# A fused local attention and MLP kernel: value tiles padded to 128 rows, one DMA for regrouped probabilities, and another order of work

## The chip, the cores and the metric

The kernel runs on one core of a Trainium2 chip. A core has five engines with instruction queues of their own: PE (TensorE, matrix products; its weight loads are listed apart as PEld), DVE (VectorE), ACT (ScalarE), POOL (GpSimd) and SP (SyncE, which here issues nearly all DMAs). Each engine works its queue in order; semaphores tie the queues together. The metric is the time of one execution on the device in microseconds (us); lower is better. Tiles in SBUF have up to 128 rows ("partitions"); PSUM holds what PE produces.

## The reference

Inputs are q, k and v (4 batches, 8 heads, 768 positions, 64 features) and two weight matrices. Attention sees a band of 31 positions around each query and, beside it, 24 block summaries (the maximum of each 32 keys, the mean of each 32 values). The result goes through an MLP with a gate of its own; all arithmetic is to float32 accuracy.

```python
k_sum = k.reshape(B, H, nb, block, D).max(axis=3)        # block = 32, nb = 24
v_sum = v.reshape(B, H, nb, block, D).mean(axis=3)
scores_l = scale * np.matmul(q, k.transpose(0, 1, 3, 2)) # kept where |i - j| < 16
scores_s = scale * np.einsum('bhsd,bhnd->bhsn', q, k_sum) + np.log(block)
a = softmax(concatenate([scores_l, scores_s]))           # with 1e-9 in the divisor
attn_out = np.matmul(a, concatenate([v, v_sum], axis=2))
x = attn_out.transpose(0, 2, 1, 3).reshape(B * S, H * D) # 3072 x 512
h = x @ w_in                                             # 512 x 2048
out = (h * erf(softplus(h))) @ w_out                     # 2048 x 512
```

## The kernel before, in words

**Tiling.** The 3072 tokens go in 6 chunks of 512. The unit of attention is a *quad*: one chunk and one pair of heads, so 24 quads, numbered `qd`. A quad has 8 groups of 64 queries; each group sees a window of 96 positions (`LW`) and 24 block sums (`NS`), 120 columns (`NK`) in all. For each quad: `scores` (PE), `softmax` (DVE: maxima and normalization; ACT: exponentials), `transp` (the probabilities are turned so that keys lie on the rows), `av` (PE: the product with the value tile `vw`), and a split of the result x into a high and a low half (`xsplit`, tiles `xh` and `xl`), since PE multiplies float32 as three products of such halves.

**Value tiles.** `vw` has 120 rows: 96 of the window, loaded from `v_win`, and 24 with the block sums (`vsum`), copied in on the chip. Quads 0 to 3 have tiles of their own (`vwf`): `load_vw_first` loads them, and the block sums come in by a copy on ACT (quad 0), by a DMA (quad 1), and by two copies on ACT that ride behind the first weight cast (`spread`, quads 2 and 3). Later quads share one tile `vw`: `load_quad_v` issues the load and, behind it on SP, one or two DMAs with the sums.

**Turning the probabilities.** Quads 0 to 7 are turned by PE and copied by ACT (`ptr`). From quad 8 on, DVE transposes blocks of 32 x 32 (`blocks`, L666), a DMA writes the result to DRAM (`out_`, L670), and four DMAs, each for 32 (the last for 24) rows, read it back regrouped (`back`, L676, tile `ptd`).

**MLP.** 24 periods (`k`), four for each chunk: `mm1` (first layer; from period 8 on replaced by `products`, which needs seven products in place of eight), softplus and erf on ACT, the gate and its split on DVE (`gsplit`), `mm2` (second layer). Weights come packed as 64-bit words and are converted at the start by three DVE operations a unit (`convert`: `a`, `b`, `c`), a cast on ACT and a subtraction on DVE (`split`: high and low half of `w`). Later, halves are kept in DRAM and read again (`w<-dr`, `ws<-ds`).

**What sets the order.** Nothing is issued as it is written. Every piece of work is entered into a plan (`P.add`) with the engines that may do it, its assumed length, and what it reads and writes. `Plan.order` then goes through time by these assumptions: on the engine that is free first it takes, of the ready pieces, the one with the smallest key, which is its due time plus a number from the table `TUNE`; a third entry picks a table set of ACT, a fourth ties a piece to one engine. DMAs are pieces of SP. The resulting sequence is issued engine by engine; waits on semaphores come from what each piece reads and writes. Before the weights are there, `busy` fills PE with matmuls on zeros (tile `idle`), at the places of the table `FILL`, after seven at the start.

**The order at the start.** PE's queue has a score piece for each of the first four quads, the block sums of V (`vs`), turns and products of the four quads, and 48 matmuls of `mm1` of period 0, 12 for each quad, which need that quad's `xh` and `xl`. DVE has the block maxima of the keys (`ksum`), the row maxima of the scores (L615) and their product with -0.125 (L631), which the exponentials (L621) need.

## Time and profile before

| what | value |
|---|---|
| time, 3 runs | 607.96, 608.32, 609.86 us; median 608.32 us |
| the profiled execution | 608.67 us, its span 606.9 us |
| PE, PEld busy | 599.3 us (99%), 498.8 us (82%) |
| DVE, ACT busy | 445.9 us (73%), 410.8 us (68%) |
| granted PE clock, mean | 0.997 |
| DMA | 166.29 MB, mean 274 GB/s |

The span runs from the first to the last instruction of one profiled execution; the time beside it also has what lies around the span. A group row has busy time, mean ns of one instruction and, behind the second bar, the idle time of the engine just before and what ended it. Busy PE time counts matmuls from issue to modelled end, so it overlaps and says little on how well PE is used. A chain row is a step on the way back from the last instruction. Line numbers are those of the kernel before; in the changed kernel the same code stands up to ten lines earlier or two later.

### The profile page before, as it was taken

The page shows a single profiled execution, that of the slowest core. Times are in us where ns is not written, and L with a number is a line of the kernel's source. Part 1 is how long each engine was busy: PE and PEld are TensorE (multiplying, and loading weights), DVE is VectorE, ACT ScalarE, POOL GpSimd, SP SyncE. Part 2 cuts the span into 40 slices and gives each one's busy share as a digit, 9 for nine tenths or more (in the row PEclk, how much of TensorE's full clock was granted, in tenths as well). Part 3 has the DMA queues.
Part 4 walks back from the last instruction along what each step waited for, and adds up shares of the span by engine and source line. Part 5 has one row for each costly group of instructions (what it writes and reads, how often), then busy time and mean ns, then how long its engine had stood idle before and what let it go on. Part 6 is the DMA issues. An engine that isn't in the chain of part 4 may idle for free.

```text
span 606.9 us, 12143 instructions
## 1 busy us (share of the span) xinstructions
PE 599.3 (99%) x4722; PEld 498.8 (82%) x4722; DVE 445.9 (73%) x910; ACT 410.8 (68%) x819; POOL 3.9 (1%) x28
## 2 busy tenths in 40 slices
PE   9899999999999999999999999999999999999997
PEld 5576566778888889889799899899898899899886
DVE  4999999977998897765979758659558547544442
ACT  5978889899968885873766964656854433542670
POOL 2000000000000000000000000000000000000000
PEclk9899999999999999999999999999999999999999
DMA  8999768759798999998989999999987773675512
GB/s 324 276 362 312 286 215 289 282 180 316 256 297 309 322 313 329 301 320 302 312 310 277 385 315 294 310 312 308 319 302 230 278 237 140 245 245 193 218 70 69
DMA packets 47380, 166.29 MB, mean 274 GB/s; under 512 B 5148, under 2 KB 17884, under 8 KB 34780
## 3 DMA queue, kind: packets, MB, share of 16 engines
q1 hardware_dynamic: 46748, 165.01, 80.3%
q8 instruction: 37, 0.61, 0.4%
q10 hardware_dynamic: 576, 0.52, 0.3%
q14 instruction: 19, 0.16, 0.1%
HBM read 131.99 MB, written 31.46 MB: 269 GB/s over the span
## 4 chain that ended last, share of the span: by engine, by line
PE 93%; DMA 6%; SPq 0%; issue 0%; DVE 0%; ACT 0%; DVEq 0%
PE ops L962 39%; PE h L807 15%; PE hb L848 15%; PE ha L848 11%; PE ops L958 5%; PE px L704 3%; PE pA L581 3%; DMA vwf<-v_win 2%; DMA dt<-ot 2%; PE px L701 2%; DMA kf<-k_nat 1%; PE pA L653 1%; DMA ptd<-dt 1%; PE idle L999 0%; PE vt L464 0%
## 5 line engine op out<-in xcount | busy, mean ns | idle before, releaser
L962 PE MATMUL ops<-w,gh 128*128 128x512 f32 x704 | 227.8, 393 | 0.0
L962 PEld LDWEIGHTS ops<-w,gh 128*128 128x128 f32 x704 | 132.5, 188 | 28.4 <-issue 1.0
L962 PE MATMUL ops<-w,gl 128*128 128x512 f32 x352 | 137.5, 391 | 0.0
L1212 ACT ACT_TABLE_LOAD x91 | 116.8, 1283 | 1.6
L938 DVE TENSOR_TENSOR hc<-wt,hc 128x1024 f32<-128x1024 f32 x44 | 52.9, 1222 | 64.9 <-ACT wt L926 64.8
L807 PE MATMUL h<-xh,w 128*128 128x512 f32 x256 | 88.6, 408 | 0.0
L279 ACT COPY hc<-hb 128x256 f32<-128x256 f32 x57 | 21.1, 371 | 97.8 <-PE hb L848 41.7
L962 PEld LDWEIGHTS ops<-w,gl 128*128 128x128 f32 x352 | 66.2, 188 | 12.4
L621 ACT ACTIVATE prx<-prx,stats 128x120 f32<-128x120 f32 x160 | 61.0, 382 | 4.1 <-DVE stats L609 3.8
L807 PEld LDWEIGHTS h<-xh,w 128*128 128x128 f32 x256 | 48.1, 188 | 12.6 <-issue 1.6
L848 PE MATMUL hb<-w,ws 128*128 128x256 f32 x384 | 56.5, 283 | 0.0
L945 DVE TENSOR_TENSOR gl<-hc,gh 128x1024 fp32r<-128x1024 f32 x44 | 53.7, 1220 | 0.7
L848 PEld LDWEIGHTS hb<-w,ws 128*128 128x128 f32 x384 | 50.8, 192 | 0.2
L807 PE MATMUL h<-xl,w 128*128 128x512 f32 x128 | 50.1, 391 | 0.0
L926 ACT ACTIVATE wt<-wt 128x1024 f32<-128x1024 f32 x48 | 49.7, 1057 | 0.4
L914 ACT ACTIVATE wt<-hc 128x1024 f32<-128x1024 f32 x32 | 32.8, 1054 | 5.6 <-DVE hc L279 5.3
L279 DVE CAST gh<-hc 128x1024 fp32r<-128x1024 f32 x38 | 26.2, 691 | 11.0 <-PE ops L962 10.5
L621 ACT ACTIVATION_READ_ACCUMULATOR prx<-prx,stats 128x1 f32 x160 | 29.9, 187 | 0.0
L958 PE MATMUL ops<-a32s,gw 128*128 128x512 f32 x64 | 29.6, 597 | 0.0
L807 PEld LDWEIGHTS h<-xl,w 128*128 128x128 f32 x128 | 24.1, 188 | 6.2 <-issue 1.4
L848 PE MATMUL ha<-w,ws 128*128 128x256 f32 x192 | 28.3, 283 | 0.0
L848 PE MATMUL ha<-xh,ws 128*128 128x256 f32 x128 | 28.2, 283 | 0.0
(167 smaller groups left out, 995.9 us busy)
## 6 DMA issues: line engine op xcount, KB each, us to landing
w<-dr SPq DMA_DIRECT2D x36, 1024.0 KB
ws<-ds SPq DMA_DIRECT2D x30, 1024.0 KB
kw<-k_win SPq DMA_DIRECT2D x20, 480.0 KB
rw<-w_in SPq DMA_DIRECT2D x8, 1024.0 KB
rw<-w_out SPq DMA_DIRECT2D x8, 1024.0 KB
dr<-w SPq DMA_DIRECT2D x8, 1024.0 KB
dt<-ot SPq DMA_DIRECT2D x16, 512.0 KB
ds<-ws SPq DMA_DIRECT2D x8, 1024.0 KB
```

The source lines that it names most:

```text
L279: e.copy(o, i) if e is nc.scalar else e.tensor_copy(o, i)
L581: nc.tensor.matmul(s["sc"][a][o, n:n + rhs.shape[-1]], lhsT=s["qb"][r, 64 * j:64 * j + 64], rhs=rhs, start=qd >= MQ, stop=True, skip_group ...
L621: nc.scalar.activation(s["pr"][:, j], s["pr"][:, j] if qd >= MQ else s["sc"][j // NI][:, i * NK:(i + 1) * NK], AF.Exp, scale=-1.0 if qd >= ...
L807: nc.tensor.matmul(hs[k, f][:, 0:T], lhsT=w[m], rhs=xt[ch, cc][x], start=(cc == 0 and n == 0), stop=(cc == 3 and n == 2))
L848: nc.tensor.matmul(shape, lhsT=w[m], rhs=y[l], start=first and c == 0 and i == 0, stop=c == 1 and i == 2, skip_group_check=True)
L914: nc.scalar.activation(wt[k, n], hc[k, n], AF.Softplus)
L926: act(0.96, lambda n=n: nc.scalar.activation(wt[k, n], wt[k, n], AF.Erf, scale=-1.0 if k < SOFT else 1.0), [s], [s], table=("sig",), after ...
L938: e.tensor_tensor(hc[k, n], wt.pop((k, n)), hc[k, n], op=ALU.mult)
L945: e.tensor_tensor(gs[k, n][1], hc.pop((k, n)), f32(gs[k, n][0]), op=ALU.subtract)
L958: nc.tensor.matmul(os_[ch, t], lhsT=x[0][:, i % 2, t * 128:(t + 1) * 128], rhs=w32["o", g, i // 2][:, i % 2], start=first, stop=last)
L962: nc.tensor.matmul(os_[ch, t], lhsT=x[y][:, i % 2, t * 128:(t + 1) * 128], rhs=w[m], start=first and n == 0, stop=last and n == 2)
L1212: nc.scalar.preload_act_table_set(sets[o["load"]])
```

## The change

1. **Value tiles of 128 rows.** `v_win` is padded with zeros on the host to 128 rows; `vwf` and `vw` have 128 rows and are loaded by DMAs over all of them. `av` reads the first 120. Since the load now writes the rows of the block sums too, what copies the sums in waits for the load. For quads 0 to 3 that is a copy on ACT (or DVE, for quad 0), or an SP DMA if the plan finds it earlier; `spread` is gone.
2. **One DMA back.** `blocks` reads the probabilities with a step of four columns, so that the four blocks interleave, and the tile comes back from DRAM by one DMA over 128 rows in place of four.
3. **Pieces joined.** The row maxima and their product with -0.125 are one piece of the plan; so are the addition of 1e-9 and the reciprocal.
4. **The plan.** The first loads get assumed times of their own (`first_dma`); the assumed landing time (`land`) counts for SP's pieces; the table `TUNE` is another one (it shows as one line below). `FILL` is gone: the fillers follow from the gaps that the plan assumes.

```diff
-TUNE = {0: (-9699.962, 1.5, 0, None), 1: (-9787.921, 1.5, 0, None), 2: (-9784.159, 1.5, 0, None),
...
-FILL = {30: 3, 48: 2, 79: 1, 81: 6, 93: 5, 91: 1, 111: 1}
+TUNE = {1: (0.9682263, 1.5, 0, None), 6: (-6.605486, 1.5, 0, None), 7: (0.7812648, 1.5, 0, None),
...
-            if e == "ACT":
+            if e == "SP":
                 end += o["land"]
...
+    def first_dma(us, fn, r=(), w=(), **kw):
+        return P.add({"SP": us}, lambda e: fn(), r, w, hold=2.0, land=-1.0, **kw)
...
-        dma(1112, go, w=[f"w{n}"])
+        if u in units[:4]:
+            first_dma(2.6, go, w=[f"w{n}"])
+        else:
+            dma(1112, go, w=[f"w{n}"])
...
-            if u == units[0]:
-                spread(2)
-                spread(3)
...
-    vws = [slot(n, [NK, 2, NB, 128], F32, "vwf") for n in W_SLOTS]
+    vws = [slot(n, [128, 2, NB, 128], F32, "vwf") for n in W_SLOTS]
...
-        dma(585, lambda: nc.sync.dma_start(out=st[p]["vw"][0:LW], in_=v_win[0, p]), w=[f"vwf{p}"])
+        first_dma(1.3, lambda: nc.sync.dma_start(out=st[p]["vw"], in_=v_win[0, p]), w=[f"vwf{p}"])
...
+        def rows_(e, p):
+            o, i = st[p]["vw"][LW:NK], vsum[LW:NK, p:p + 1, :].to_broadcast([NS, NB, 128])
+            e.dma_start(out=o, in_=i) if e is nc.sync else copy(e, o, i)
         for p in range(NP):
-            if p == 0:
-                on({"DVE": 1.13, "ACT": 0.95}, lambda e: copy(e, st[0]["vw"][LW:NK], vsum[LW:NK, 0:1, :].to_broadcast([NS, NB, 128])), ["vsum00"], ["vwg0"])
-            else:
-
-                dma(100, lambda p=p: p == 1 and nc.sync.dma_start(out=st[p]["vw"][LW:NK], in_=vsum[LW:NK, p:p + 1, :].to_broadcast([NS, NB, 128])), [f"vsum0{p}"], [f"vwg{p}"])
+            on({"ACT": 0.95, "SP": 0.45} if p else {"DVE": 1.13, "ACT": 0.95}, lambda e, p=p: rows_(e, p), [f"vsum0{p}", f"vwf{p}"], [f"vwg{p}"])
...
-            s["vw"] = sb([NK, NB, 128], F32, "vw")
-            nc.sync.dma_start(out=s["vw"][0:LW], in_=v_win[ch, p])
+            s["vw"] = sb([128, NB, 128], F32, "vw")
+            nc.sync.dma_start(out=s["vw"], in_=v_win[ch, p])
...
+            e.tensor_scalar(s["mx"], s["mx"], -0.125, None, op0=ALU.mult)
...
+            e.reciprocal(s["rs"], s["rs"])
...
-            on({"DVE": 1.14}, red, banks, [f"mx{par}"])
-            on({"DVE": 0.07}, lambda e: e.tensor_scalar(s["mx"], s["mx"], -0.125, None, op0=ALU.mult), [f"mx{par}"], [f"mx{par}"])
+            on({"DVE": 1.3}, red, banks, [f"mx{par}"])
...
-            e.transpose(out=s["ot"].rearrange("p k j q -> p j k q"), in_=prx.rearrange("p j (k q) -> p j k q", k=4))
+            e.transpose(out=s["ot"].rearrange("p k j q -> p j k q"), in_=prx.rearrange("p j (q k) -> p j k q", k=4))
...
-            for k in range(4):
-                n = min(32, NK - 32 * k)
-                e.dma_start(out=s["pt"][32 * k:32 * k + n].rearrange("p a j q -> p a (j q)"), in_=s["dt"][:, 0:n, k].rearrange("a p f -> p a f"))
+            e.dma_start(out=s["pt"].rearrange("p a j q -> p a (j q)"), in_=s["dt"].rearrange("a p k f -> (p k) a f"))
...
-                        nc.tensor.matmul(xo[r, o], lhsT=s["vw"][:, j, r], rhs=s["pt"][:, j % 2, b:b + 64], start=True, stop=True)
+                        nc.tensor.matmul(xo[r, o], lhsT=s["vw"][0:NK, j, r], rhs=s["pt"][0:NK, j % 2, b:b + 64], start=True, stop=True)
...
-                busy(FILL.get(o["n"], 0))
+                busy(int(max(0.0, o["start"] - last) / 0.31))
...
-    v_win = np.ascontiguousarray(windows(v).transpose(0, 2, 4, 1, 3, 5)).reshape(NCH, NP, LW, NB, 128)
+    v_win = np.zeros((NCH, NP, 128, NB, 128), dtype=f)
+    v_win[:, :, :LW] = windows(v).transpose(0, 2, 4, 1, 3, 5).reshape(NCH, NP, LW, NB, 128)
```

How the order moves, at the places that matter at the start. **SP, the first loads**, before (`kf`, `qf`: keys and queries of a quad; `vt`: V by tokens, for its block sums; `rw`: a packed unit of weights):

```order
L495 DMA vt<-v_tok 128x3x512
L490 DMA kf<-k_nat 128x768
L491 DMA qf<-q_t 128x512
L315 DMA rw<-w_in 128x2048
L498 DMA vwf<-v_win 96x1024
L315 DMA rw<-w_in 128x2048
L498 DMA vwf<-v_win 96x1024
L519 DMA vwf<-vsum 24x8x128
L315 DMA rw<-w_in 128x2048
L498 DMA vwf<-v_win 96x1024
```

Ahead of these rows stand, in this order, `qf`, `kf`, `qf`, `kf`, `vt`, `kf`, `qf`. With the change:

```order
L491 DMA kf<-k_nat 128x768 x2
L492 DMA qf<-q_t 128x512
L496 DMA vt<-v_tok 128x3x512 x2
L317 DMA rw<-w_in 128x2048
L499 DMA vwf<-v_win 128x1024
L492 DMA qf<-q_t 128x512
L499 DMA vwf<-v_win 128x1024
L317 DMA rw<-w_in 128x2048
L499 DMA vwf<-v_win 128x1024
L317 DMA rw<-w_in 128x2048 x2
L499 DMA vwf<-v_win 128x1024
```

Ahead of these rows stand `kf`, `qf`, `kf`, `qf`. A key load is first now, the third transfer is the second key load (the fourth before), the last query load stands behind the first `vwf`, the second `vwf` ahead of the second `rw`, and no copy of block sums stands in between.

**ACT, from the third quad's exponentials on**, before (`vwf<-vsum`: block sums into a value tile; `ptr`: turned probabilities; `w<-a`: weight cast; `xh`: high half of x):

```order
L511 COPY vsum<-vs 24x512
L279 COPY vwf<-vsum 24x1024
L658 COPY ptr<-pA 120x512
L658 COPY ptr<-pB 120x512
L621 ACTIVATE prf,stats<-h_302,stats 128x120 x4
L621 ACTIVATE prf,stats<-h_303,stats 128x120 x4
```

And with the change:

```order
L512 COPY vsum<-vs 24x512
L281 COPY vwf<-vsum 24x1024
L651 COPY ptr<-pA 120x512
L651 COPY ptr<-pB 120x512
L281 CAST w<-a_320 128x1024
L281 COPY vwf<-vsum 24x1024
L281 CAST xh<-px 128x512
L615 ACTIVATE prf,stats<-h_322,stats 128x120 x4
```

The first weight cast, the second value tile's sums and quad 0's high half now stand ahead of quad 3's exponentials.

**DVE, the first rows**, before and with the change (`ksum`: block maxima of the keys; `stats<-h`, `stats<-pA`: row maxima of the scores; the TENSOR_SCALAR: the product with -0.125):

```order
L501 TENSOR_REDUCE ksum<-kf 128x24 x2
L615 TENSOR_REDUCE stats<-h_140 128x4
L615 TENSOR_REDUCE stats<-h_141 128x4
L615 TENSOR_REDUCE stats<-pA 128x4
L615 TENSOR_REDUCE stats<-pB 128x4
L631 TENSOR_SCALAR stats<-stats 128x8 x2
```

```order
L502 TENSOR_REDUCE ksum<-kf 128x24 x2
L608 TENSOR_REDUCE stats<-pA 128x4
L608 TENSOR_REDUCE stats<-pB 128x4
L609 TENSOR_SCALAR stats<-stats 128x8
L502 TENSOR_REDUCE ksum<-kf 128x24
```

The product of the first quad stood behind the maxima of two quads; now it follows its own.

More of the change, by code (lines that the diff above doesn't have):

```diff
@@ L489, in load_qk_first @@
         st[p] = dict(qb=qfs[:, p], vw=vws[p // 2][:, p % 2])
-        dma(480, lambda: nc.sync.dma_start(out=kfirst[p], in_=k_nat[0, p]), w=[f"kf{p}"])
-        dma(330, lambda: nc.sync.dma_start(out=qfs[:, p], in_=q_t[0, p]), w=[f"qf{p}"])
+        first_dma(0.97, lambda: nc.sync.dma_start(out=kfirst[p], in_=k_nat[0, p]), w=[f"kf{p}"])
+        first_dma(0.66, lambda: nc.sync.dma_start(out=qfs[:, p], in_=q_t[0, p]), w=[f"qf{p}"])
     def load_v_first():
         for n in range(2):
-            dma(786, lambda n=n: nc.sync.dma_start(out=vts[n], in_=v_tok[3 * n:3 * n + 3].rearrange("t s c -> s t c")), w=[f"vt{n}"])
+            first_dma(2.0, lambda n=n: nc.sync.dma_start(out=vts[n], in_=v_tok[3 * n:3 * n + 3].rearrange("t s c -> s t c")), w=[f"vt{n}"])
     def load_vw_first(p):
-        dma(585, lambda: nc.sync.dma_start(out=st[p]["vw"][0:LW], in_=v_win[0, p]), w=[f"vwf{p}"])
+        first_dma(1.3, lambda: nc.sync.dma_start(out=st[p]["vw"], in_=v_win[0, p]), w=[f"vwf{p}"])
     def ksum_first(p):
@@ L629, in softmax @@
         else:
-            on({"DVE": 1.14}, red, banks, [f"mx{par}"])
-            on({"DVE": 0.07}, lambda e: e.tensor_scalar(s["mx"], s["mx"], -0.125, None, op0=ALU.mult), [f"mx{par}"], [f"mx{par}"])
+            on({"DVE": 1.3}, red, banks, [f"mx{par}"])
         s["exps"] = act(3.02 if qd >= MQ else 2.7, exps, [f"mx{par}"] + ([pr] if qd >= MQ else list(banks)), [pr, f"sm{par}"], table=("log", "exp"))
-        on({"DVE": 0.07}, plus, [f"sm{par}"], [f"rs{par}"])
-        on({"DVE": 0.11}, lambda e: e.reciprocal(s["rs"], s["rs"]), [f"rs{par}"], [f"rs{par}"])
+        on({"DVE": 0.21}, plus, [f"sm{par}"], [f"rs{par}"])
         def norm(e):
@@ L673, in back @@
             s["pt"] = sb([128, 4, 2 * NI, 32], F32, "ptd", "pt")
-            for k in range(4):
-                n = min(32, NK - 32 * k)
-                e.dma_start(out=s["pt"][32 * k:32 * k + n].rearrange("p a j q -> p a (j q)"), in_=s["dt"][:, 0:n, k].rearrange("a p f -> p a f"))
+            e.dma_start(out=s["pt"].rearrange("p a j q -> p a (j q)"), in_=s["dt"].rearrange("a p k f -> (p k) a f"))
         on({"DVE": 1.14}, blocks, [pr], ["ot"])
-        on({"SP": 1.43}, out_, ["ot"], [f"dt{qd % 2}"], hold=0.3, land=3.6)
-        on({"SP": 3.0}, back, [f"dt{qd % 2}"], ["pt"], hold=0.3, land=3.0)
+        on({"SP": 1.43}, out_, ["ot"], [f"dt{qd % 2}"], hold=0.3, land=0.6)
+        on({"SP": 1.9}, back, [f"dt{qd % 2}"], ["pt"], hold=0.3, land=0.4)
     turned = [0]
@@ L692, in go @@
         def go():
-            assert qd >= NP or qd in filled
             xo = s["xo"] = ps("px", bank)
@@ L700, in go @@
                         b = 64 * (NI * a + j // 2)
-                        nc.tensor.matmul(xo[r, o], lhsT=s["vw"][:, j, r], rhs=s["pt"][:, j % 2, b:b + 64], start=True, stop=True)
+                        nc.tensor.matmul(xo[r, o], lhsT=s["vw"][0:NK, j, r], rhs=s["pt"][0:NK, j % 2, b:b + 64], start=True, stop=True)
                     else:
                         z = 2 * (j % 2)
-                        nc.tensor.matmul(xo[r, o].rearrange("d (a q) -> d a q", a=2), lhsT=s["vw"][:, j, r], rhs=s["pt"][0:NK, z:z + 2, NI * a + j // 2], start=True, stop=True)
+                        nc.tensor.matmul(xo[r, o].rearrange("d (a q) -> d a q", a=2), lhsT=s["vw"][0:NK, j, r], rhs=s["pt"][0:NK, z:z + 2, NI * a + j // 2], start=True, stop=True)
         pe(1.08, go, ["pt", "vw"] if qd >= NP else ["pt", f"vwf{qd}", f"vwg{qd}"], [bank])
@@ L1204, in block_attention_mlp @@
     sets = {"exp": "exp_and_others", "log": "natural_log_exp_and_others", "sig": "sigmoid_and_others", "soft": "softplus"}
-    filling = True
+    filling, last = True, free["PE"]
     for o in plan:
@@ L1209, in block_attention_mlp @@
             if filling:
-                busy(FILL.get(o["n"], 0))
+                busy(int(max(0.0, o["start"] - last) / 0.31))
+            last = o["end"]
         if "load" in o:
```

8 lines of the change are left out of this document (1 added, 7 removed).

## The prediction, made before the result was known

> **What bounds the kernel now.** I read the page first (busy time by engine), then a table of stretches, then the chain of waits, then the instructions of the first 42 us engine by engine. The page, and the stretches (start:end, length, then busy us of PE, PEld, DVE, ACT and POOL with their counts, the granted PE clock, the DMA engines' share, GB/s):
>
> ```profile
> PE 599.3 (99%) x4722; PEld 498.8 (82%) x4722; DVE 445.9 (73%) x910; ACT 410.8 (68%) x819; POOL 3.9 (1%) x28
> ...
> 0.00:16.00 16.00, 14.88 (x242) 8.35 (x243) 7.54 (x18) 8.45 (x35) 3.86 (x28) 1.00 0.90 328
> 16.00:36.00 20.00, 18.35 (x265) 12.67 (x264) 18.93 (x28) 18.44 (x58) 0.00 (x0) 0.91 1.02 273
> 36.00:50.00 14.00, 13.94 (x115) 10.74 (x113) 13.48 (x16) 9.47 (x12) 0.00 (x0) 1.00 1.01 402
> 50.00:120.00 70.00, 70.00 (x471) 45.15 (x462) 69.27 (x140) 61.82 (x125) 0.00 (x0) 1.00 0.79 274
> 120.00:228.00 108.00, 108.00 (x750) 87.53 (x747) 95.00 (x196) 93.03 (x168) 0.00 (x0) 1.00 0.82 282
> 318.00:603.00 285.00, 285.00 (x2140) 255.50 (x2136) 175.26 (x361) 160.40 (x296) 0.00 (x0) 1.00 0.75 251
> ```
>
> Two limits follow each other. From 318 us PE alone is the bound (DVE 175 of 285 us). From 16 to 120 us DVE is busy too: 18.93 of 20, 13.48 of 14, 69.27 of 70 us. In the first 16 us DVE works 7.54 us only. So what the start loses on DVE stays lost: PE cannot make it up later. A busy PE is not a useful PE either; the chain of waits (start, us, what) tells more:
>
> ```profile
> 7.42 14.17 DMA vwf<-v_win
> 22.43 1.12 issue
> 23.55 0.80 PE px L701 x19
> ...
> 29.71 4.10 PE h L807 x18
> ...
> 35.51 2.94 PE h L807 x12
> ...
> 39.67 1.58 PE h L807 x6
> 41.49 7.74 PE h L807 x33
> 50.21 0.91 PE h L807 x3
> ...
> 581.47 21.80 PE ops L962 x96
> ```
>
> The start hangs on the first window load of V. The gap of 1 us at 49.2 is one of several before 228 us. The last row gives PE's true price: 21.80 / 96 = 0.227 us a matmul; the tail behind it (603.27 to 606.9) keeps its form.
>
> **The start, step by step.** DVE and ACT now (start, us, what; in brackets the idle time and what ended it):
>
> ```profile
> 4.51 0.95 DVE L501 TENSOR_REDUCE ksum<-kf 128x24 f32<-128x768 f32 x1 [3.37 <-DMA kf<-k_nat]
> 7.43 0.95 DVE L501 TENSOR_REDUCE ksum<-kf 128x24 f32<-128x768 f32 x1 [1.97 <-DMA kf<-k_nat]
> 8.30 1.21 DVE L615 TENSOR_REDUCE stats<-h 128x4 f32<-128x480 f32 x2
> 10.55 0.29 DVE L631 TENSOR_SCALAR stats<-stats 128x8 f32<-128x8 f32 x2
> 20.12 0.69 DVE L332 TENSOR_SCALAR a<-rw 128x1024 uint32<-128x1024 uint32 x1
> 25.98 0.69 DVE L332 TENSOR_SCALAR a<-rw 128x1024 uint32<-128x1024 uint32 x1 [0.90 <-DMA rw<-w_in]
> 37.41 1.22 DVE L357 TENSOR_TENSOR w<-a,w 128x1024 fp32r<-128x1024 f32 x1
> 38.55 1.22 DVE L335 SCALAR_TENSOR_TENSOR a<-rw,a 128x1024 uint32<-128x1024 uint32 x1
> 39.80 1.23 DVE L338 SCALAR_TENSOR_TENSOR a<-rw,a 128x1024 uint32<-128x1024 uint32 x1
> 40.94 0.68 DVE L720 TENSOR_TENSOR xl<-px,xh 128x512 fp32r<-128x512 f32 x1
> ...
> 10.81 0.36 ACT L621 ACTIVATE prf<-h,stats 128x120 f32<-128x120 f32 x1 [6.36 <-DVE stats L631]
> 19.18 0.58 ACT L511 COPY vsum<-vs 24x512 f32<-24x512 f32 x1
> 19.79 1.04 ACT L279 COPY vwf<-vsum 24x1024 f32<-24x1024 f32 x1
> ```
>
> The first exponentials wait for the multiplication by -0.125 at 10.55, which stands behind both quads' maxima (8.30 to 10.5). Everything after them (24 exponentials up to the copy at 19.18, 2.7 us a quad, then transposes) is late with them, and DVE starts converting weights at 20.12.
>
> **Maxima and key loads.** The multiplication now follows its own quad's maxima, and the key load that holds DVE is the third transfer, not the fourth. Bytes decide when that lands: 1.31 MB stood up to it, now 1.05 MB. At the first row's rate, with nothing in the first 2 us and about 300 GB/s to 6 us, 1.05 MB is moved at 5.2 us; a landing is seen 0.6 to 1.3 us after its bytes (the loads seen at 4.51 and 7.43 had 0.66 and 1.31 MB up to them, moved at 3.9 and 6.1), I take 1.0: 6.2 us. Then a reduction (0.9), two maxima (1.15) and the product (0.15): exponentials from 8.4, 2.4 us earlier. Three quads take them to 16.6, the copy of the V sums to 17.2. The folded pairs of small operations remain the same instructions: nothing.
>
> **The V load.** SP's issues now:
>
> ```profile
> 7.42 0.35 SPq L498 DMA_DIRECT2D vwf<-v_win  x1
> 19.78 0.98 SPq L519 DMA_DIRECT2D vwf<-vsum  x1
> ...
> 14.00:16.00 2.00, 2.00 (x16) 1.02 (x11) 1.84 (x5) 2.00 (x14) 0.00 (x0) 1.00 1.07 422
> 22.00:24.00 2.00, 0.88 (x25) 0.79 (x25) 2.00 (x4) 2.00 (x13) 0.00 (x0) 1.00 1.07 246
> 24.00:26.00 2.00, 2.00 (x31) 1.28 (x26) 1.10 (x3) 1.46 (x8) 0.00 (x0) 0.62 0.99 276
> ```
>
> Up to the first weight unit 5.24 MB are issued, all over 128 partitions, and 328 GB/s x 16 us = 5.25 MB: it has just arrived when the first 96-row V load's turn comes. From there to 36 us the engines are as busy (1.02) but move 273 GB/s, and beyond 36 us, with the V loads through, 402 again. In these 20 us the four V loads (1.57 MB) share 5.46 MB; at 0.41 MB/us these take 13.3, so 6.7 us are lost, 1.7 per V load. I therefore price a 128-row load by its bytes at 0.41 MB/us (0.52 MB, 1.3 us); the other end is 273 GB/s for everything, as now.
>
> Up to the first V load the new order issues 5.51 MB: moved at 16.6, seen at 17.6 instead of 21.6. The second (6.29 MB) is seen at 19.5, the weight units 0 to 3 (4.98, 7.34, 8.91, 9.96 MB) at 16.4, 22.0, 25.7, 28.2. SP no longer waits for the sums (its copy stood at 19.78).
>
> **What the padding costs on ACT.** The load now fills the rows of the sums too, so the four copies of the sums must wait for it, on ACT, in order. Behind the first copy stand the two copies of the transposed probabilities, and PE's first product waits for those. ACT is free at 17.2, waits to 17.6, copies to 18.7 and 19.7. PE has its scores of quad 3 done by 19.5 (the last query load, 5.77 MB, is seen at 18.2), so the product runs 19.8 to 20.9; now it starts behind the load, at 21.6, and ends at 24.4. ACT pays one copy more (1.04 us), inside this sum.
>
> **The sum at 42 us.** DVE can convert from 16.4 (weight unit 0 seen; its two normalizations end at 15.5), not from 20.12. From there to the last low half of x (xl of quad 3) it has, by the pitches of the rows above, four conversions (0.6 + 1.25 + 1.14 each, 12.0 us), three low halves of weights (1.14 each, 3.4), four of x (0.6 each, 2.4), a cast of x (0.6), normalization, maxima and small ones (2.8), and two block sums of the next batch (1.7) that now come later: 22.9 us without a wait, since ACT's inputs come 0.4 to 1.6 us ahead of each use. It ends at 39.3, now at 41.6 (the row at 40.94), and is 1.7 us of other work ahead: DVE leads by 4.0 us. PE's row for the wait behind that half:
>
> ```profile
> 41.68 0.50 PE L807 MATMUL h<-xl,w 128*128 128x512 f32 x1
> ```
>
> All 36 matmuls that need nothing of quad 3 are done before it (the 18, 12 and 6 of the chain). In the new order they are too: the products of quads 0 to 3 end at 20.9, 27.5, 33.0 and 37.3, and the 36 at 39.3 (on ACT the exponentials of quad 3 end at 25.1, the copies for quad 1 at 26.1, a normalization and a weight cast at 29.6, the copies for quads 2 and 3 at 30.6 and 35.3; a product needs 1.1 us behind its copies, that of quad 3 also nine matmuls ahead of it, of which three wait for quad 2's half). So PE is 2.4 us ahead at the same point, DVE 4.0. Until 120 us both are full; there the 1.6 us that DVE is further ahead can close gaps of PE like the one at 49.2, half of it I count: 2.4 + 0.8 = 3.2 us.
>
> **The clock.** 26 filling matmuls become 18. After 20 to 24 us, where PE worked 2.41 of 4 us with no gap over 1.2 us, the clock fell to 0.62. My PE is idle for 1.7 us before the scores of quad 3, and as sparse up to 24. The cost lies between nothing (PE waits for ACT and DVE anyway) and 3 us (PE's 3 us there at half speed, and some 13 matmuls); 0.5 taken, near the lower end, since DVE sets the pace. [...]
>
> **Steady work.** Three edits, each hidden. The rows are a stretch while the regrouped probabilities come back in four partial loads, the issues of these, the only PE wait for them, the transposes, and SP's longest wait:
>
> ```profile
> 328.00:329.00 1.00, 1.00 (x10) 1.00 (x10) 1.00 (x2) 0.54 (x2) 0.00 (x0) 1.00 1.07 148
> 324.63 1.71 SPq L676 DMA_DIRECT2D ptd<-dt  x4
> PE px L704 <- DMA ptd<-dt: 1.1, 1, 1.1
> L666 DVE STREAM_TRANSPOSE ot<-prx x16: 1233/1238/1246, 132.8 to 468.3; 128x1024 f32<-128x1024 f32 x16
> SPq L381 <- PE ops L962: 88.9, 19, 6.5
> ```
>
> One load over all partitions saves SP about 1.3 us a quad and lifts a dip of 148 GB/s; PE waited 1.1 us once, so 0 to -1.1, and 0 taken, as a new order can put such a wait elsewhere. The transposes read with a step of four elements, which no row shows; conversions that read every second word cost 1.2 us like plain ones. The bounds are nothing and a doubling, the distance between the two forms of conversion (0.69 and 1.22 us for the same 1024 elements): up to 16 x 1.24 = 19.8 us, which lies in DVE's idle 13 us (120 to 228) and 110 us (318 to 603); without that cover it would be paid in full. The copies of the sums behind each V load now wait on SP for it (20 times), with weight reloads and query and key loads behind them, which PE waits for. One landing is 1.3 + 1.0 us, on a queue that waits 88.9 us for PE to free weight buffers: 0 on the path, 1 us at most in all. 0.13 MB more per V load (20 times) is 6 us at 0.41 MB/us, in a DMA share of 0.75.
>
> Sum: -3.2 + 0.5 = -2.7 us. The profiled execution took 608.67 us (span 606.9), 0.35 over the median of 608.32; against the median the forecast is 605.6.
>
> **The rivals.** (1) *The padding does not speed the load.* For: the slow stretch also holds a 24-row copy of the sums, which I cannot separate from the loads. Against: the rate returns as the V loads end. At 273 GB/s the weight units 1 to 3 are seen at 24.7, 30.4, 34.3, DVE waits 3 us for them and xl of quad 3 ends at 42.9, 1.3 later than now, with 1.7 of block sums done ahead: at worst 1.3 lost on PE, half of DVE's 0.4 regained, less than 0.3%: 608.8 with nothing else moved, no change. [...]
>
> (2) *ACT is held: slower.* If the slow stretch goes by bytes and a padded load is a third longer there, 5.6 us (16 to 21.6) become 7.5 and the first V load is seen at 23.5. ACT, in order, holds both transposed copies, and everything behind moves by 5.9 us less the 0.4 us spare: 3.2 - 5.5 = 2.3 lost, 610.6. The gain is gone from a landing at 21.2 on. Against: the same as for (1).
>
> (3) *More comes with it.* The gaps before 228 us (like that at 49.2) arise where DVE is full; with 4.0 us of DVE's lead passed on whole, that gap of 1.0 closed and the 1.1 us wait with it, 6.1 us go: 602.2.
>
> **How the numbers follow.** A measurement of this kernel can tell about 0.3% (1.8 us) from no change. The forecast 0.50 (its own range 603.2 to 606.4), (3) 0.16, (1) 0.22, (2) 0.12. Faster is the forecast and (3), 0.66; same is (1), 0.22; slower is (2), 0.12. The range 601 to 609 holds the forecast with the clock's 3 us, (1), and (3) with the clock's half us back and some more; it leaves (2) out.
>
> **What would show it.** Exponentials from about 8.4; first V load seen before 18.5; about 400 GB/s from 16 to 28 us; DVE converting from about 16.5; xl of quad 3 ending near 39.3; a granted clock near 1 there; transposes between 1.24 and 2.5 us; PE from 318 us as before. It is wrong if ACT waits over 4 us for the first V load, if DVE waits for weights, or if a lead of over 2 us at 42 us is there and PE gives it back before 318.

## The result, and the profile after

The changed kernel takes 613.41 us (median of 5 executions, 611.56 to 613.56), the kernel before, beside it on the same chip, 608.32 (607.47 to 610.76): a ratio of 1.0066 worked out from all executions (the medians alone would give 1.0084), 95% interval 1.0038 to 1.0093. It is slower by 0.7%. The forecast was 605.6 with a range of 601 to 609. The profiled execution of the changed kernel took 612.39 us, its span is 610.2.

The table of stretches, with the columns of the one in the prediction (start:end, length, busy us of PE, PEld, DVE, ACT and POOL, granted PE clock, DMA share, GB/s), changed kernel:

```profile
0.00:16.00 16.00, 11.30 (x226) 6.70 (x227) 8.53 (x19) 9.44 (x39) 3.83 (x28) 0.98 0.89 327
16.00:36.00 20.00, 18.73 (x234) 11.48 (x233) 17.50 (x26) 16.59 (x51) 0.00 (x0) 0.93 0.97 393
120.00:228.00 108.00, 108.00 (x759) 87.27 (x758) 98.33 (x197) 91.02 (x164) 0.00 (x0) 1.00 0.80 292
318.00:603.00 285.00, 285.00 (x2163) 255.11 (x2162) 178.67 (x355) 157.60 (x297) 0.00 (x0) 1.00 0.70 250
12.00:14.00 2.00, 0.00 (x0) 0.00 (x0) 1.08 (x2) 2.00 (x14) 0.00 (x0) 1.00 1.07 422
14.00:16.00 2.00, 1.82 (x4) 0.78 (x5) 1.45 (x5) 1.74 (x11) 0.00 (x0) 0.86 0.98 403
16.00:18.00 2.00, 2.00 (x4) 0.94 (x3) 1.93 (x4) 2.00 (x13) 0.00 (x0) 0.50 1.06 409
```

The queue does what was foreseen: 393 GB/s from 16 to 36 us, before 273. PE does not: in the first 16 us it works 11.30 us (before 14.88), from 12 to 14 us nothing at all, and behind that the granted clock is 0.50. The chain of waits of the start, and its last row, name it:

```profile
3.54 6.90 DMA qf<-q_t
...
10.57 1.41 PE o L574 x58
11.98 2.20 issue
14.18 0.23 PE o L574
14.41 7.05 PE vs L508 x12
21.47 0.02 issue
21.49 0.59 ACT vsum L512
...
584.75 21.80 PE ops L952 x96
```

Between the last two matmuls of the block-key scores of quad 2, PE stands for 2.20 us, and no instruction that the profile shows releases it ("issue"). Then the twelve matmuls of the V sums take 7.05 us, and ACT's copy of these sums, with everything that stands behind it, starts at 21.49; the prediction had it at 16.6. The last 96 matmuls start at 584.75, before at 581.47: 3.28 us later, which is the whole difference of the spans (610.2 less 606.9). DVE and ACT at the places that the prediction named:

```profile
7.18 0.95 DVE L502 TENSOR_REDUCE ksum<-kf 128x24 f32<-128x768 f32 x1 [2.54 <-DMA kf<-k_nat]
9.57 0.36 ACT L615 ACTIVATE prf<-pA,stats 128x120 f32<-128x120 f32 x1 [5.13 <-DVE stats L609]
18.25 0.69 DVE L337 TENSOR_SCALAR a<-rw 128x1024 uint32<-128x1024 uint32 x1
21.49 0.58 ACT L512 COPY vsum<-vs 24x512 f32<-24x512 f32 x1 [3.23 <-PE vs L508]
42.97 0.68 DVE L710 TENSOR_TENSOR xl<-px,xh 128x512 fp32r<-128x512 f32 x1
L659 DVE STREAM_TRANSPOSE ot<-prx 128x1024 f32<-128x1024 f32 x16 | 32.9, 2056 | 0.3
PE hb L838 <- DVE stats L602: 1.0, 1, 1.0
SPq L549 <- DMA vw<-v_win: 42.4, 15, 5.9
```

The last low half of x comes 2.0 us later than before, not 2.3 earlier. The last three rows are the steady work: the stepped transposes take 2.06 us instead of 1.24, PE has a new wait of 1.0 us for VectorE's maxima (at 300 us), SP waits 42.4 us for padded V windows.

**Where the time is lost.** The products of probabilities and V are good milestones, one a quad. Start of the last matmul of some of them, in us, one profiled execution each, with those of the experiments below; from quad 13 on, the same matmuls stand behind the milestone in all of them, so differences there are PE's lead or lag.

| kernel | quad 0 | quad 3 | quad 13 | quad 14 | quad 15 | quad 20 | quad 23 |
|---|---|---|---|---|---|---|---|
| before | 24.1 | 39.5 | 269.6 | 295.4 | 318.9 | 435.4 | 503.3 |
| changed | 25.1 | 41.6 | 272.4 | 297.0 | 321.7 | 438.7 | 506.5 |
| e1, fillers | 23.7 | 40.1 | 271.0 | 295.6 | 320.3 | 437.2 | 505.1 |
| e2, paired scores | 22.6 | 38.7 | 270.4 | 294.9 | 319.6 | 436.6 | 504.4 |
| e3, plain transposes | 22.8 | 39.3 | 272.0 | 296.6 | 320.5 | 437.1 | 504.9 |
| e9, one pair | 21.5 | 38.1 | 268.8 | 293.4 | 318.2 | 435.1 | 503.0 |
| e10, before with part 2 | 24.6 | 39.5 | 269.5 | 294.4 | 319.7 | 436.6 | 504.8 |
| e14, step alone | 23.7 | 38.1 | 268.5 | 294.4 | 318.6 | 435.5 | 503.7 |
| e15, one load alone | 24.4 | 39.5 | 269.7 | 294.3 | 318.8 | 435.3 | 503.2 |

The changed kernel is 2.1 us late at quad 3, 2.8 at quads 13 and 15, 3.2 at quad 23. So two thirds of it are lost in the first 42 us, and 1.1 us later. One execution is not exact at the start: the kernel before, e10, e14 and e15 have the same program up to quad 8, and their quad 3 stands at 38.1 to 39.5, so a lead of up to 1.4 us there can be chance. Two theories follow. *Code*: the 2.20 us are PE's next instructions, not yet there. *Clock*: PE works too sparsely from 6 to 14 us with its fewer fillers, and the low clock is the cause. A third, *steady*, looks for the loss in the stepped transposes and SP's waits.

### The profile page after: what moved, and what is told of

It is laid out like the page before. It is cut to its first block, busy times and chain, and to the rows that moved or that the text cites. A ratio compares the mean times of both kernels' runs of the same rounds, so it can differ in the third digit from the quotient of the medians.

```text
span 610.2 us, 12059 instructions
## 1 busy us (share of the span) xinstructions
PE 599.5 (98%) x4714; PEld 498.1 (82%) x4714; DVE 460.5 (75%) x915; ACT 407.9 (67%) x815; POOL 3.8 (1%) x28
## 4 chain that ended last, share of the span: by engine, by line
PE 94%; ACT 2%; DVE 1%; DMA 1%; issue 1%; SPq 0%; ACTq 0%
PE ops L952 39%; PE hb L838 15%; PE h L797 14%; PE ha L838 11%; PE ops L948 5%; PE pA L574 3%; PE px L694 3%; PE vs L508 1%; DMA qf<-q_t 1%; PE px L691 1%; ACT prf L615 0%; ACT ptr L651 0%; PE pA L646 0%; ACT w L281 0%; PE pB L574 0%
## 5 line engine op out<-in xcount | busy, mean ns | idle before, releaser
L797 PE MATMUL h<-xh,w 128*128 128x512 f32 x256 | 86.8, 402 | 0.0
L281 ACT COPY hc<-hb 128x256 f32<-128x256 f32 x56 | 20.8, 371 | 85.5 <-DVE hc L891 31.3
L281 DVE CAST gh<-hc 128x1024 fp32r<-128x1024 f32 x40 | 27.5, 688 | 11.2 <-PE ops L952 10.7
L659 DVE STREAM_TRANSPOSE ot<-prx 128x1024 f32<-128x1024 f32 x16 | 32.9, 2056 | 0.3
L797 PEld LDWEIGHTS h<-xl,w 128*128 128x128 f32 x128 | 24.1, 188 | 6.0 <-DVE xl L710 1.0
```

The costliest lines, as they stand in the source:

```text
L281: e.copy(o, i) if e is nc.scalar else e.tensor_copy(o, i)
L659: e.transpose(out=s["ot"].rearrange("p k j q -> p j k q"), in_=prx.rearrange("p j (q k) -> p j k q", k=4))
L797: nc.tensor.matmul(hs[k, f][:, 0:T], lhsT=w[m], rhs=xt[ch, cc][x], start=(cc == 0 and n == 0), stop=(cc == 3 and n == 2))
```

## The experiments

Every label is run against the kernel before. Medians in us, ratios with 95% intervals; the ratios are worked out from all executions and differ from the quotient of the medians by up to 0.2%.

**1. Is the hole code, or is it the clock?** Part 3 of the changed kernel's profile page has a queue for instructions; the second row is what that queue moved from 11.4 to 11.6 us (packets, MB, share of the 16 engines), where it is seen for the first time.

```profile
q8 instruction: 37, 0.61, 0.4%
q8 instruction: 1, 0.02, 32.6%
```

37 packets with 0.61 MB are some 16 KB each; if the queue is PE's alone, the 4714 matmuls and 4714 weight loads that the page counts make 255 a packet, an estimate from these numbers. e1 adds fillers, which moves the hole if it hangs on the count, and keeps PE busier.

```
-                busy(int(max(0.0, o["start"] - last) / 0.31))
+                busy(int(max(0.0, o["start"] - last) / 0.31) + {28: 3, 36: 3}.get(o["n"], 0))
```

> Six filling matmuls more, three ahead of the scores of quad 1 and three ahead of those of quad 2, where PE of the changed kernel waits 0.8 and 0.6 us for query loads. Theory 'code' (the 2.2 us without work at 12.0 us, labelled issue, are PE's next packet of code, 16 KB on queue q8, that starts at 11.4 and is needed at 12.0; the slow clock only follows from the hole): the hole stays, about 2 us long, six matmuls earlier in the program (before the 26th of the 32 block-key matmuls of quad 2 and not before the last), the granted clock falls to 0.5 to 0.8 behind it, the twelve matmuls for the V sums end at 20.8 to 21.6, time 613 (within 2 us of the changed kernel). Theory 'clock' (the clock falls because PE has fewer fillers and works sparsely from 6 to 11 us): granted clock 1.00 from 14 to 20 us, the V sums take 5.6 and not 7.1 us, end at 20.0, time 611.5 to 612.

Measured: 611.64, 1.0029 (1.0003 to 1.0055). PE's rows in e1 around the hole, and the instructions counted up to it, in e1 and in the changed kernel:

```profile
11.28 0.60 PE L574 MATMUL o<-ksum,qf 64*64 64x24 f32 x25
14.34 0.31 PE L574 MATMUL o<-ksum,qf 64*64 64x24 f32 x7 [2.47 <-issue]
0.00:14.20 14.20, 10.82 (x222) 6.50 (x222) 6.52 (x13) 8.14 (x33) 3.86 (x28) 1.00 0.87 319
```

```profile
0.00:14.10 14.10, 9.49 (x222) 5.92 (x222) 7.08 (x14) 7.79 (x31) 3.83 (x28) 1.00 0.88 317
```

The hole stands behind the same count, 222 matmuls and 222 weight loads (in e3 and e4 too), and so six matmuls earlier in the program: behind the 25th and not the 31st. It is 2.47 us long in e1, 2.20 in the changed kernel, and its end follows the packet: in the changed kernel, e1, e3 and e4 the packet is counted between 11.0 and 12.0 us, and PE goes on 2.3 to 2.7 us after it. The kernel before has its hole of 1.12 us at 22.43 in the same way, one packet later (counted from 20.8 to 21.0 us): up to the end of it 347 matmuls and 348 loads are counted, 251 more.

```profile
0.00:23.50 23.50, 20.79 (x347) 11.79 (x348) 14.94 (x31) 15.84 (x65) 3.86 (x28) 1.00 0.93 309
```

So the hole is code: e2 and e9, below, take it away by moving that count behind longer work. The 251 from one hole to the next agree with the 255 a packet. In the changed kernel the packet was first counted at most 0.6 us before it was needed (11.4 and 11.98 us).

The clock is a second cost on top. Every execution has a mean granted clock. The profiled executions of the kernel before and the changed kernel, at 0.997 and 0.996, show 0.57 over 4 us (24 to 28 and 15 to 19 us); those of e1, e3 and e9, at 1.000, show 1.00 from 14 to 20 us. So 0.997 or less is read here as a fall; where it is, only a profiled execution shows. It fell in all 5 executions of the changed kernel and all 10 of e4. In e3 (section 3), which has the same start with the same 18 fillers, it fell in 5 of 10; in e1, with 24 fillers, also in 5 of 10. In e1 those five took 611.8 to 612.4, the five others 609.9 to 611.5. The profiled executions of e1 and e3 are among the others: they have the hole and keep the clock. These are e3's rows:

```profile
13.56 0.23 PE L574 MATMUL o<-ksum,qf 64*64 64x24 f32 x1 [1.99 <-issue]
13.73 5.41 PE L508 MATMUL vs<-vt,pick 128*120 128x512 f32 x12
14.00:20.00 6.00, 6.00 (x30) 2.62 (x31) 5.76 (x13) 4.17 (x22) 0.00 (x0) 1.00 1.02 409
```

So the hole does not come from the clock. That fewer fillers bring the low clock is not shown, since e3 keeps it as often as e1 without them. The kernel before pays for the clock too, in fewer executions: beside e1 to e4 it fell in 11 of 31, median 610.5 against 608.2.

e2 takes 48 matmuls out from ahead of the V sums:

```
-            pe(0.5, lambda: keys(lambda r, j: [(LW, ksum[r, 0, qd])]), ...)
+            pe(0.5, pairs, ...)      # one matmul for 128 queries: lhsT=s["qb"][r, 128*i:128*i+128], rhs=ksum[r, 0, qd]
```

> The scores against the block keys take 128 queries at a time: 16 matmuls in place of 32 for each of the first four quads, same result; 48 matmuls fewer stand ahead of the V sums, nothing else moves. Theory 'code': the packet that starts at 11.4 us is then first needed 48 matmuls later, after the V sums: no hole of over 0.5 us before 16 us, granted clock 1.00, V sums from 11.9 to 17.6 (now 14.4 to 21.5), first product ends near 21.5 (now 25.3), last low half of x near 40 (now 43.6), time 609 to 610, 3.5 to 4.5 us less than the changed kernel. Theory 'clock': hole of 2 us gone or not, the clock still falls near 14, V sums take 7 us, gain 2 us at most: 611.5. Theory 'steady' (what costs the time is the stepped transposes and SP's waits for the padded V loads; a lead at 42 us is given back): first product early, but time 613.

Measured: 609.96, 1.0002 (0.9975 to 1.0028). No hole before 22 us, the clock fell in 2 of 10 executions, first product 2.5 us earlier than in the changed kernel, last low half of x from 40.1. But the wide matmuls are slower: of the two rows, the first is e2's, the second the kernel before's (the same work).

```profile
8.56 1.07 PE L585 MATMUL h<-ksum,qf 64*128 64x24 f32 x16
```

```profile
6.97 0.67 PE L581 MATMUL h<-ksum,qf 64*64 64x24 f32 x32
```

e9 therefore pairs the scores of quad 1 alone (16 matmuls fewer are enough, since the V sums that follow are long matmuls, twelve in 5.38 us), and takes e4's loads (below).

```
-            pe(0.5, pairs, ...)
+            pe(0.5, pairs if qd in (1,) else lambda: keys(lambda r, j: [(LW, ksum[r, 0, qd])]), ...)
-            nc.sync.dma_start(out=s["vw"], in_=v_win[ch, p])
+            nc.sync.dma_start(out=s["vw"][0:LW], in_=v_win[ch, p, 0:LW])
```

> The changed kernel with the block-key scores of quad 1 alone taken by 128 queries (16 matmuls fewer ahead of the V sums; in the kernels with all four paired, the 16 wide matmuls took 1.07 us where the 32 narrow ones took 0.67), and V windows of the later quads over 96 partitions. Theory 'code': 16 matmuls are enough, since the packet of code is then first needed behind the twelve long matmuls of the V sums: no hole over 0.5 us before 18 us, granted clock 1.00 in most executions, first product ends by 23, time 608.5 to 609.5. Rival 'width' (what helped was the paired form in all quads, not the count): hole of 2 us still there, 612.

Measured: 608.96, 1.0010 (0.9994 to 1.0027). PE and ACT of e9:

```profile
11.25 0.67 PE L574 MATMUL o<-ksum,qf 64*64 64x24 f32 x32
12.50 5.38 PE L508 MATMUL vs<-vt,pick 128*120 128x512 f32 x12 [0.59 <-DMA vt<-v_tok]
17.92 0.58 ACT L512 COPY vsum<-vs 24x512 f32<-24x512 f32 x1 [0.90 <-PE vs L508]
18.53 1.04 ACT L281 COPY vwf<-vsum 24x1024 f32<-24x1024 f32 x1
20.48 1.28 PE L697 MATMUL px<-ptr,vwf 120*64 120x64 f32 x32
39.46 0.68 DVE L716 TENSOR_TENSOR xl<-px,xh 128x512 fp32r<-128x512 f32 x1
```

No hole; V sums in 5.38 us, not 7.05; the clock fell in 2 of 12 executions. The table has e9 3.5 us ahead of the changed kernel at quad 3 and 3.5 ahead at quad 23: a lead or a lag of the start stays to the end, as PE has no spare time. Hole and clock together are worth 3.5 us of the profile. Against e4, which has the same loads, they are worth 2.8 us of the median, or 2.3 by the two ratios (the two ran on different chips). e1 and e3, with the hole and the full clock, stand between at quad 3: some 1.2 to 2.0 of the 3.5 us are the hole's, the rest the clock's.

**2. Does the padding speed the load, and does that help?** e8 is e2 with the first four V windows over 96 partitions.

```
-        first_dma(1.3, lambda: nc.sync.dma_start(out=st[p]["vw"], in_=v_win[0, p]), ...)
+        first_dma(1.3, lambda: nc.sync.dma_start(out=st[p]["vw"][0:LW], in_=v_win[0, p, 0:LW]), ...)
```

> The changed kernel with paired scores, but the first four V windows over 96 partitions as before the change (their block-sum rows then need no wait). Theory 'padding speeds the queue': the rate from 16 to 36 us falls from about 400 to about 280 GB/s, the V window of quad 0 is seen 1 to 2 us later than the 19.1 us of the paired kernel and the weight units 1 to 3 by 2 to 6 us, DVE waits for them, 611 to 613 (paired kernel 610). Rival 'bytes': the rate stays near 400, everything is seen at the same time or earlier, 609 to 610.

Measured: 615.82, 1.0115 (1.0096 to 1.0133). The stretch from 16 to 36 us, e2 first, then e8:

```profile
16.00:36.00 20.00, 18.49 (x253) 12.62 (x252) 18.71 (x26) 18.40 (x49) 0.00 (x0) 1.00 1.00 398
```

```profile
16.00:36.00 20.00, 17.42 (x208) 12.14 (x209) 15.65 (x22) 14.94 (x45) 0.00 (x0) 0.83 1.02 304
```

With fewer bytes the queue moves 304 instead of 398 GB/s. Neither kernel has a copy of the sums on this queue in these 20 us, so the loads alone do it: the padding does speed the queue, as forecast. Why short loads slow the queue is not shown. (e8 loses another 3.5 us at 245 to 320 us to late readbacks and reloads; why these come with it is not shown.)

e6 and e7 ask the same of the old order. e6 is the kernel before with e2's pairs; e7 adds the padded first windows, with the copies of the sums on ACT behind their loads:

```
-        dma(585, lambda: nc.sync.dma_start(out=st[p]["vw"][0:LW], in_=v_win[0, p]), ...)
+        dma(585, lambda: nc.sync.dma_start(out=st[p]["vw"], in_=v_first[p]), ...)      # v_first: 128 rows
-            if u == units[0]:
-                spread(2)
-                spread(3)
+            if u == units[2]:
+                spread(3)      # spread(1) and spread(2) behind the copies of their transposed probabilities
```

> The kernel before with the block-key scores of the first four quads by 128 queries (64 matmuls fewer in all), nothing else. Theory 'code': its own hole of 1.1 us at 22.4 us moves to a later place and shrinks, the slow clock at 24 to 28 us behind it goes in most executions; but PE waits there for the V load and for ACT anyway, so 0 to 1 us less, 607.5 to 608.5, with fewer of the executions at 610 to 611. Theory 'start set by the V load alone': no difference, 608.5, hole or not.

> The kernel before with paired scores and one part of the change: the first four V windows padded to 128 rows and loaded over all partitions, each block-sum copy on ACT behind its load (quad 0 where it was, quads 1 and 2 behind the copies of their transposed probabilities, quad 3 behind the cast of the third weight unit). Theory 'padding speeds the queue' (the prediction's): about 400 GB/s from 16 to 28 us in place of 273, V window of quad 0 seen at 19 to 19.5 (before 21.6), first product by 22, last low half of x near 40 (before 41.6), 606 to 607.5. Rival 'bytes' (a padded load only moves a third more): V window at 21.6 or later, ACT held, 609 to 610.

Measured: e6 609.13, 1.0018 (1.0006 to 1.0030); e7 610.38, 1.0039 (1.0026 to 1.0053). The rate rises as in the new order, 287 to 414 GB/s, but the first product of e7 is not earlier (24.9, in e6 23.8): ACT reaches the copy of the sums at 21.28, and no engine of e7 waits for the V window. The faster load by itself buys nothing in the old order. In the kernel before PE had waited for it 0.5 us, and right behind that stood ACT; in e6 already no engine waits for it. (e7's first exponentials stand at 12.92, in e6 at 11.86; why is not shown. That 1.1 us is the whole distance of the first products, and makes the 1.2 us of the medians unclear; the lack of a gain does not hang on it.)

**3. The steady work.** e3 undoes part 2 in the changed kernel, e4 the padding of the later windows (edit shown with e9).

```
-  in_=prx.rearrange("p j (q k) -> p j k q", k=4)
+  in_=prx.rearrange("p j (k q) -> p j k q", k=4)
-  e.dma_start(out=s["pt"]..., in_=s["dt"].rearrange("a p k f -> (p k) a f"))
+  for k in range(4):      # four loads of 32, 32, 32 and 24 partitions, as before
```

> The transposes of VectorE read as before the change (key = 32 k + p, neighbouring elements), and the readback is four loads of 32, 32, 32 and 24 partitions again; order and start as in the changed kernel. Theory 'start' (code or clock): transposes 1.24 us again and DVE 13 us less busy, but time 613, within 0.3%. Theory 'steady': 3 us less, 610; and if the four loads cost more than the transposes save, up to 614.

> The V windows of the later quads (20 loads) are loaded over 96 partitions again, so the copies of the block sums on SP need not wait for them; the first four stay padded, everything else as in the changed kernel. Theory 'start': SP's waits for V windows (42 us in all now) are gone, time 613, within 0.3%. Theory 'steady' in the form 'SP is held': 1 to 3 us less. [...]

Measured: e3 611.21, 1.0039 (1.0008 to 1.0071), with the low clock in 5 of 10 executions; e4 611.78, 1.0048 (1.0023 to 1.0074), with the low clock in all. In e4 the waits of SP for V windows are gone and its milestones stay 0.2 to 0.3 us ahead of the changed kernel's throughout: these 42.4 us of SP cost next to nothing. In e3 PE waits 1.5 us for the four-part readback, and 0.3 instead of 1.0 us for the maxima at 300 us: two costs that trade. Against e1, whose profile has the hole and the full clock too, e3 loses 1.8 us from quad 3 to 13 and gains 1.2 from there to quad 23; at the full clock e3's median is 610.4, e1's 610.0. So e10 puts part 2 alone into the kernel before, and e14 and e15 each half of it (`(q k)` in the transposes; the one load).

> The kernel before with one part of the change: VectorE's transposes read with a step of four elements, and the regrouped probabilities come back by one load over 128 partitions (before: four loads of 32, 32, 32 and 24). Theory 'hidden': transposes 2.06 us each (13 us more DVE in all) cost nothing, and the waits of 1.1 us for the partial loads near 290 us go: 607 to 608, ratio 0.998 to 1.000. Rival 'transposes cost': 0.5 to 3 us more, 609 to 611.

> The kernel before with the stepped reading of VectorE's transposes alone; the readback stays four loads, so the keys of quads 8 to 23 reach the second product in another order than the rows of V (the result is not the reference's; the work is the same). Theory 'stride' (the step costs the kernel what it lost with both parts): transposes 2.06 us, PE's wait for VectorE's maxima near 300 us about 1.7 us or, where the readback's own wait of 1.1 us comes first, 0.6 to 1.7 us: 609 to 611. Theory 'readback' (the loss comes from the one load arriving earlier or from its place in the queues): 608.3, as before.

> The kernel before with the one readback over 128 partitions alone and plain transposes (again with the keys of quads 8 to 23 out of order, so the result is not the reference's). Theory 'stride': the 1.0 us gained near 290 us stays: PE waits for the readback 0 instead of 1.1 us, for VectorE's maxima near 300 us 0.5 us at most, 607 to 607.8. Theory 'readback': 609.5 to 610.5, as with both parts.

Measured: e10 610.31, 1.0031 (1.0018 to 1.0045); e14 609.85, 1.0021 (1.0006 to 1.0035); e15 608.72, 1.0005 (0.9994 to 1.0017). The step costs, the one load neither costs nor gains. PE's waits of e10, e14 (two rows) and e15, and the stretch from 296 to 304 us of the kernel before and of e10:

```profile
PE hb L846 <- DVE stats L609: 1.7, 1, 1.7
296.00:304.00 8.00, 6.31 (x39) 5.49 (x38) 7.93 (x27) 3.88 (x19) 0.00 (x0) 1.00 0.81 264
```

```profile
PE px L704 <- DMA ptd<-dt: 1.0, 1, 1.0
PE hb L848 <- DVE stats L609: 0.6, 1, 0.6
```

```profile
PE hb L846 <- DVE stats L609: 0.9, 1, 0.9
```

```profile
296.00:304.00 8.00, 8.00 (x49) 7.08 (x48) 7.90 (x28) 3.82 (x19) 0.00 (x0) 1.00 0.99 356
```

In the kernel before DVE is busy 7.90 of these 8 us; PE just keeps up. In e15 PE comes there 1.0 us earlier (its wait for the readback is gone) and waits 0.9 for DVE: the gain is given back on the spot. In e10 one transpose of 2.0 us stands in that stretch in place of 1.2, so PE waits 0.8 more. The table shows both: at quad 14 e10 and e15 are 1.0 and 1.1 us ahead of the kernel before, at quad 15 e15 is level and e10 0.8 behind. e10 and e14 lose 0.4 more between quads 15 and 20 and 0.3 from there to quad 23, e15 nothing: 1.5 to 1.6 us of loss behind quad 13 that only the kernels with the step have.

Two further kernels were to have plain transposes and one load together, by storing in four pieces:

```
+            for k in range(4):
+                e.dma_start(out=s["dt"][k].rearrange("p a f -> a p f"), in_=s["ot"][:, k].rearrange("p j q -> p (j q)"))
+            e.dma_start(out=s["pt"]..., in_=s["dt"].rearrange("k p a f -> (k p) (a f)"))
```

> The kernel before with one readback of the regrouped probabilities over 128 partitions, but plain transposes: they go out in four stores over 128 partitions (one for each group of 32 keys, so that the keys lie in order in DRAM) and come back in one load. Theory 'stride' (the 1.8 us that the kernel before loses near 300 us with the stepped transposes, where PE waits 1.7 us for VectorE's maxima, come from the 0.82 us that each transpose is longer; the 1.0 us that it gains near 290 us come from the one load): the gain stays and the loss goes: transposes 1.24 us, the wait of PE for the maxima near 300 us at most 0.5 us, 607 to 607.6, ratio 0.998 to 0.9995. Rival 'order of arrival' (the loss comes from anything that is 1 us earlier at 290 us and then waits at 300): 608.3 or more.

> The changed kernel with the scores of quad 1 paired and V windows of the later quads over 96 partitions (608.96 before this edit), and now plain transposes with four stores and one load. Theory 'stride': the wait of 1.0 us of PE for VectorE's maxima near 300 us shrinks to 0.3 or less, no wait for the readback comes in its place, 608.0 to 608.5. Rival: the four stores hold SP and the readback comes late, 609 to 610.

Measured: e12 616.54, 1.0134 (1.0112 to 1.0157); e13 629.48, 1.0348 (1.0318 to 1.0378). The stores themselves came late (in e12 SP waits 36.3 us for them and PE 2.7 for the readback, in e13 PE waits 6.6 us for block sums queued behind them). They settled nothing on the step; e14 and e15 did.

**4. Put together.** e5 is e2 with e1's fillers and e4's loads; e11 is e10 with the scores of quads 2 and 3 paired.

> Three edits of the changed kernel together: block-key scores by 128 queries, six fillers in PE's two first waits, V windows of the later quads over 96 partitions. Theory 'offset' (PE has no spare time behind 42 us, so what the start gains is kept): the start of the kernel with paired scores (last low half of x at 40 us), granted clock 1.00 in nearly all executions, and the wait of 0.8 us for a weight reload near 250 us gone since SP no longer waits for V windows: 608.8 to 609.3, about level with the kernel before. Rival 'loads' (behind 240 us the weight reloads set the pace once PE is 3 us earlier): the wait stays, 609.5 to 610.

> The kernel before with that part, and the block-key scores of quads 2 and 3 by 128 queries, so that its own hole of 1.1 us in the first product (at 22.4 us, with the slow clock of 24 to 28 us behind it) falls into a place where PE waits anyway. Theory 'code': no hole over 0.5 us, granted clock 0.999 or 1 in nearly all executions and not in two of three, 606.5 to 608. Rival: the wider matmuls put 0.4 us on each of two quads' scores and the start is 0.5 to 1 us later, 608.5 to 609.

Measured: e5 610.04, 1.0029 (1.0018 to 1.0040), low clock in 0 of 6 executions; e11 610.31, 1.0027 (1.0014 to 1.0040), low clock in 2 of 12, no hole over 0.3 us, and e10's wait of 1.7 us. e5 shows a spread that no edit explains: up to its second reduction of keys its loads are those of the changed kernel and e2, and the third transfer is seen at 7.37 us, in e2 at 6.45 (the two rows, e5 first).

```profile
7.37 0.95 DVE L502 TENSOR_REDUCE ksum<-kf 128x24 f32<-128x768 f32 x1 [2.45 <-DMA kf<-k_nat]
```

```profile
6.45 0.95 DVE L502 TENSOR_REDUCE ksum<-kf 128x24 f32<-128x768 f32 x1 [1.63 <-DMA kf<-k_nat]
```

No version beat the kernel before; e9, which mends the hole, is level with it, and so are e2 and e15 (each interval holds 1).

## Why the prediction was wrong, point by point

- **Rate of the queue: right.** 393 GB/s from 16 to 36 us where some 400 were forecast; e8 shows that the padding does it. Rival (1), that it does not, falls.
- **Exponentials from 8.4: right in kind.** 9.57 in the changed kernel, 8.64 in e9. The third transfer, forecast at 6.2, was seen at 7.18 and over all nine profiles of this order at 6.20 (e13) to 7.37 (e5): a landing worked out from bytes alone has that spread.
- **V sums copied from 17.2, first product 19.8 to 20.9: wrong, and this is the step that failed.** The prediction let PE run its scores and the V sums as soon as their data were there; PE's own supply of instructions was put at nothing, without a reason. In the new order the scores of three quads, all short matmuls (32 in 0.67 us in e9's row), stand ahead of the long V sums, so PE is through the 222 matmuls and 222 weight loads ahead of the hole by 11.98 us and stands until 14.18. The V sums start at 14.41 in place of 12.50 (e9) and then take 7.05 us in place of 5.38, with a granted clock of 0.50 from 16 to 18 us; ACT's copy starts 3.6 us later than in e9 (21.49, 17.92). Mended in e9, the first product runs 20.48 to 21.8, and the last low half of x ends at 40.1 (forecast 39.3). The "issue" row of 1.12 us in the kernel before's chain was quoted in the prediction and not asked what it was.
- **The clock at +0.5: mis-sized and misplaced.** It was priced where PE waits anyway, at 20 to 24 us. It fell at 15 to 19 us (0.57 granted), where PE is the chain. Within one kernel (e1) it is worth 1.9 us of the median. The clock fell behind a hole of 2.20 us in the changed kernel, and stayed at 1.00 behind 2.47 us in e1's profile and 1.99 in e3's. In the kernel before it had fallen to 0.62 at 24 us behind a gap of 1.12 us, as the prediction noted.
- **The lead of 2.4 us on PE and 0.8 from DVE: mis-sized.** With the hole mended, PE goes on behind the last low half of x at 40.1 instead of 41.7, and with DVE both block sums ahead; but by quads 13 and 15 its lead on the kernel before is 0.8 and 0.7 us, at quad 23 0.3. DVE's 1.7 us of work done ahead closed no gap of PE that the table shows. Even the lead of 1.4 us at quad 3 is no more than the old start varies (e14 is level with e9 there, at 38.1). That PE keeps a lead or lag is right (e9 against the changed kernel: 3.5 us at quad 3 and at quad 23).
- **The start "hangs on the first window load of V": too shallow.** The chain showed it, but only 0.5 us deep: e7 loads faster and gains nothing.
- **Stepped transposes hidden in DVE's idle 13 and 110 us: wrong in place.** Idle time of DVE over 108 or 285 us is no cover at 300 us, where DVE is busy 7.90 of 8; the stretch from 228 to 318 us is not in the prediction's table at all. The step costs 0.8 us there and 0.7 later (e14: 1.0021). In the changed kernel PE's wait of 1.0 us at 303 us is this place; e3, which takes the step out, pays as much for the four-part readback.
- **SP's waits for V windows at 0: right** (e4), though they are 42.4 us.
- **Rival (2), ACT held by the V load, 610.6:** right in direction and wrong in cause: ACT waited 3.23 us for PE's V sums, not for the load. Rival (3) needed a lead that the changed kernel never had.
- Sum of the profile, by milestones against the kernel before: start without the hole 1.4 us ahead at quad 3 (e9), hole and clock 3.5 behind, 1.1 lost between quads 3 and 23, of which 0.5 behind quad 13: 3.2, and the spans differ by 3.3. What takes the 0.6 us between quads 3 and 13, where the two orders differ, is not shown.

Open: why the clock falls in all executions of the changed kernel and e4 and in half of e3's and e1's, though all have the hole; e3 has even the same fillers and the same program up to quad 8.

## What to carry to other kernels

When an order of work puts many short matmuls at the start of a program, count instructions, not only microseconds: here an "issue" gap of 2.20 us on PE, at 11.98 us, behind a packet that an instruction queue moved from 11.4 to 11.6, was code that was not there yet, and the cure was to have long instructions run at that count (in e9, 16 short ones fewer were enough). Price an off-path edit in the stretch where it runs, a few us wide, not by an engine's idle time over a hundred. A chain of waits names what ended last, not by how much: before pricing the removal of a wait, look at how long the waiting engine stood there, and who comes second.
